# The last weight but one, loaded half in whole rows and half in column halves

## The chip, the cores and the metric

The kernel runs on one core of a Trainium2 chip. The metric is the device time of one execution in microseconds. Before the change it is 147.64 us, the median of three runs that lie between 147.49 and 147.65. One further execution was recorded by the hardware profiler, and all rows of the profile are of that one.

## The reference

An attention stage feeds a mixture of experts with soft slots. Cut to what matters:

```python
# attention: B=4, H=8, S=768, D=64; per head either full causal or sinks plus a window of 64
a = softmax(mask(q @ k.T / 8)); x = (a @ v) as [3072, 512]
# soft slots: NE=8 experts, 4 slots each, D=512, F=1024
logits = x @ phi                                   # [3072, 32]
slot_input = softmax(logits, axis=0).T @ x         # [8, 4, 512]
for e in range(8):
    slot_out[e] = relu(slot_input[e] @ w1[e]) @ w2[e]   # w2[e] is [1024, 512]
out = softmax(logits, axis=1) @ slot_out           # [3072, 512], fp32
```

The weights w1 and w2 are 2 MB of fp32 for each expert, 32 MB in all; the output is 6.29 MB of fp32.

## The kernel before

**Order.** The kernel describes its work as a list of named operations, each with an engine, an estimated duration, a key (a due time), the operations that it depends on and the buffers that it takes and frees. A planner (`Plan.run`) simulates the engines and emits the instructions in the order that it finds. What an engine does is therefore fixed at build time; at run time an engine only waits for semaphores, in that order. The function `dma` describes a load: an "issue" operation on GpSimd (POOL), chained to the load issued before it and to the landing of the load eight places earlier, and a "land" operation with the estimated transfer time, which the consumers depend on.

**Loads.** All inputs but three small ones are loaded by DMAs that POOL issues, one after the other on one queue, and the DMA converts them from fp32 to bf16 on the way. The weights are numbered: w0 to w7 are the experts' w1, w8 to w15 their w2. A whole w2 is laid out with the partition as `fi` and eight rows `fo` in each partition (row 8*fi + fo), so that a partition reads contiguous rows of 512 fp32 values, 2 KB each. The last two weights, w14 and w15 (experts 6 and 7), are split: `load_half(i, c)` loads the 256 columns of half c for all eight `fo`, 1 KB read and 512 B written at a time. The issue order at the end is w11, w12, w13, then w14.0, w15.0, w14.1, w15.1. These go into memory that the attention stage has done with: `pt` for w14, `qk` for w15, `xv` for w13, `vx` for w12.

**The experts.** The hidden layer comes first (H, the relu HR, the transposes TH, their copies HE). Then the second products: `w2_op(e, c0, c1)` makes W2.e for both halves at once (eight matmuls of 512 columns, one for each `fo`) or W2.e.c for one half (eight of 256). They add up in one PSUM bank, `so`, for all experts, since each slot's hidden values are masked to its expert. For each half: W2.6.c, the filling products ZT (three of zeros for half 0, two for half 1, made by `wait_zeros`, result unused), W2.7.c, and the scaling SO.c, which turns the half of the bank into bf16 `slot_out`.

**The output.** The 24 output tiles are a product of a 128x128 block of `expT` with `slot_out` (OM), scaled while it is moved out of PSUM by DVE or ACT (OE), with reciprocals that DVE makes of row sums (RW0, RW1 on PE, RWR0, RWR1 on DVE; RW1 is made in the right half's turn). Twelve tiles are done in column halves, first their left halves and after W2.7.1 their right halves; the other twelve are done whole at the end. The stores of the left halves are two on POOL's queue (128 KB and 384 KB) and four on SP's (256 KB each); then follow six right ones of 256 KB and three of 1 MB for the whole tiles, all on SP, which issues them in this order.

Of the kernel before, what the change touches and what calls it, by code (L numbers as in the profile page):

```python
# [226 lines left out]
def kernel(  # L227
# [19 lines left out]
    NE, DM, F = moe_w1.shape  # L247
# [61 lines left out]
    def tr_bf(s, n):  # L309
# [9 lines left out]
    hT_t = [xbf[:, 1024 * e:1024 * (e + 1)].rearrange("p (f c) -> p f c", f=8) for e in range(2)]  # L319

    pl = Plan({"S8": 11, "QT": 2, "KT": 2, "VT": 1, "VB": 2, "VF": 3, "PT": 2, "PTX": 2, "XB": 2,
               "XT": 1, "SC": 2, "TR": 2, "PV": 1, "BK": 8})
# [6 lines left out]
    def on(eng, occ, late=0.18):  # L329
        return {eng: (occ, occ + late)}  # L330
# [12 lines left out]
    def dma(name, nbytes, buf, dst, src, deps=()):  # L343
        if len(chain) >= 8:
            deps = list(deps) + [chain[-8]]
        iss = pl.op("issue " + name, on("POOL", 0.645, 1.4), -100, deps=list(deps) + [fifo[0]],
                    acq=[buf] if buf else [], lead=1.3, emit=lambda o: nc.gpsimd.dma_start(dst(), src))  # L347
        fifo[0] = iss
        took = nbytes / (395000.0 if nbytes == 1 << 20 and name != "w0" else 423000.0)
        chain.append(pl.op("land " + name, {"DMA": (took, took + 1.85 + 0.05 * len(chain))}, -100, deps=[iss] + chain[-1:], lead=5.2))  # L350
        return chain[-1]

# [23 lines left out]
    NW, NSPLIT = 2 * NE, 2  # L376
    wbuf = [Buf("S8") for _ in range(NW)]
    wland = [None] * NW
    late_mem = {}
# [6 lines left out]
    def w_row(i, x):  # L386
        n = 2 if i < NE else 4
        return w_mem(i)[:, x // n, :].rearrange("p (a f) -> p a f", a=n)[:, x % n, :]

    def w_half(i, c):  # L390
        return late_mem[i]()[:, 2048 * c:2048 * (c + 1)].rearrange("p (a f) -> p a f", a=8)

    hland = {}

    def load_half(i, c, deps=()):
        src = moe_w2[i - NE].rearrange("(fi fo) d -> fi fo d", fo=8)[:, :, 256 * c:256 * (c + 1)]
        hland[i, c] = dma(f"w{i}.{c}", 1 << 20, None, lambda: w_half(i, c), src, deps=deps)

    def load_w(i, deps=()):
        if i == 0:  # L400
# [124 lines left out]
    for n in range(4):  # L525
        o_fm[n] = pl.op(f"fm{n}", on("ACT", 0.65) if n == 0 else on("POOL", 0.9), -8 if n == 0 else T * n - 3.5,
                        deps=[o_fl], emit=lambda o, n=n: head_flags(o, n))
# [15 lines left out]
    def phi_t2(o):  # L543
        for n in range(4):
# [8 lines left out]
                  emit=lambda o: nc.vector.tensor_copy(  # L553
                      phi4, tr_bf(pb2.slot, 4 * NS).rearrange("p (n r s) -> p n r s", n=4, r=1).to_broadcast(
                          [P, 4, 4, NS])))
# [3 lines left out]
    def load_tile(ti):  # L559

        tbuf[ti], tland[ti], p0 = Buf("S8"), [], 0
        for x, b, x0, x1 in TILES[ti]:
# [8 lines left out]
                  emit=lambda o, x=x: nc.gpsimd.tensor_copy(w_mem(0)[:, 0, KB * x:KB * (x + 1)],  # L571
                                                            w0f[:, KB * x:KB * (x + 1)])) for x in range(4)]
# [116 lines left out]
    for b in range(B):  # L689
        for n in range(4):  # L690
            p = 4 * b + n
# [4 lines left out]
            def emit_v2(o, n=n, tr=tr):  # L696
                t = tr_bf(tr.slot, 768)
                for j in range(6):
                    nc.tensor.transpose(t[:, 128 * j:128 * (j + 1)], vT[:, 6 * n + j, :], ident)  # L699

            a = pl.op(f"V2.{p}", pe(56, 6), k0 + 1.5, deps=evs("v", b, n), acq=[tr], rel=[VTb[b]],
                      emit=emit_v2, mode="full", mm=6)

            def emit_vb(o, b=b, n=n, tr=tr):
# [4 lines left out]
                           acq=[VBb[b]] if n == 0 else [], rel=[tr], emit=emit_vb)  # L709
            VFb[p] = Buf("VF")  # L710

            def emit_vf(o, b=b, n=n, p=p):
# [4 lines left out]
                           emit=emit_vf)  # L717

            PTb[b, n] = Buf("PT")
            for kk, g in enumerate(range(5)):  # L720
# [3 lines left out]
                def emit_qk(o, b=b, n=n, g=g, sc=sc):  # L724
                    parts, c = [], 0
                    for j, q0, nb in PGROUPS[g]:
# [4 lines left out]
                a = pl.op(f"QK.{p}.{g}", on("PE", 0.235, 0.26), key - 2.0, deps=evs("q", b, n) + evs("k", b, n),  # L731
                          acq=[sc], rel=[QTb[b], KTb[b]], emit=emit_qk, mode="r64", mm=2 * len(PGROUPS[g]))

                def emit_ex(o, b=b, n=n, g=g, sc=sc):
# [4 lines left out]
                                   acq=[PTb[b, n]] if kk == 0 else [], rel=[sc], emit=emit_ex)  # L739
                for m, gs in enumerate(MGROUPS):  # L740
                    if gs[-1] == g:
                        o_m = pl.op(f"MK.{p}.{m}", on("DVE", [0.605, 0.605, 0.335][m]), key + 0.3,
                                    deps=[expo[p, x] for x in gs] + [o_hm[n]], emit=mask_emit(b, n, m))
# [3 lines left out]
        for ns in ([(0, 1), (2, 3)] if b == 0 else [(0, 1, 2, 3)]):  # L747
# [18 lines left out]
            def emit_mx(o, b=b, ns=ns):  # L766
# [5 lines left out]
                      emit=emit_mx)  # L772
# [5 lines left out]
    for b in range(B):  # L778
        for n in range(4):
            p = 4 * b + n  # L780
# [162 lines left out]
        if b == B - 1:  # L943
# [29 lines left out]
    load_w(12, deps=[pv_ops[f"PV.{p}.5"] for p in range(8, 12)])  # L973
    load_w(13, deps=[pv_ops["DS.2"]] + [pv_ops[f"XT.{p}"] for p in range(8, 12)] +
           [pv_ops[f"V2.{p}"] for p in range(12, 16)])
    load_half(14, 0, deps=[pv_ops["PV.14.5"]])
    load_half(15, 0, deps=qk_done[3])
    load_half(14, 1)
    load_half(15, 1)
# [68 lines left out]
    w2o = {}  # L1048

    def w2_op(e, c0, c1):  # L1050
        def emit_w2(o):
            e4, g0 = e // 4, e % 4
            for fo in range(8):
                g = fo % 4
                nc.tensor.matmul(banks[so.slot][32 * g:32 * (g + 1), 256 * c0:256 * c1],
                                 hT_t[e4][:, fo, 32 * g0:32 * (g0 + 1)], w_row(NE + e, fo) if c1 - c0 == 2 else w_half(NE + e, c0)[:, fo, :],
                                 start=(e == 0 and fo < 4), stop=(e == NE - 1 and fo >= 4),
                                 tile_position=(0, 32 * g), skip_group_check=True)

        land = [wland[NE + e]] if c1 - c0 == 2 else [hland[NE + e, c0]]  # L1060
        o = pl.op(f"W2.{e}" + ("" if c1 - c0 == 2 else f".{c0}"), on("PE", 0.22 * (c1 - c0), 0.27),
                  kt + (29 + e if c0 == 1 else 16 + e),
                  deps=[hte[e // 4]] + land + [w2o[c] for c in range(c0, c1) if c in w2o],
                  acq=[so] if e == 0 else [], emit=emit_w2, mode="c32", mm=8)
        for c in range(c0, c1):
            w2o[c] = o

# [6 lines left out]

        pl.op(name, pe(190, n), key, deps=[dep], acq=[zw] if first else [], rel=[zw], emit=emit_z, mode="full", mm=n)

    for e in range(NE - NSPLIT):
        w2_op(e, 0, 2)
    whole = w2o[0]
    for c in range(2):  # L1080
# [141 lines left out]
```

## Time and profile before

| What | Value |
|---|---|
| median of three runs | 147.64 us (147.49 to 147.65) |
| profiled execution | 147.56 us |
| its span on the core | 145.8 us, 4941 instructions |
| PE, DVE, ACT, POOL busy | 85%, 76%, 74%, 28% of the span |
| DMA queue q0 (POOL's) | 26.22 MB, its packets 92.9% of the 16 engines' time |
| DMA queue q1 (SP's) | 6.88 MB, 12.7% |
| granted clock of PE, mean | 0.944 |

The span runs from the first to the last instruction of the program; the rest of the execution's time lies around it. In the rows of the timeline the first column is the start in us from the span's start, the second the duration; PEld is PE's load of weights. In the rows of stretches the busy time of each engine stands in us with its number of instructions. The bytes of a converting load are counted as written, that is in bf16. A DMA's row has the size that it writes and the time from its issue to its landing.

### The profile page before, as it was taken

How to read it: one execution, taken by the hardware profiler on the slowest of the kernel's cores; microseconds unless marked ns; L12 is line 12 of the kernel's file. 1: busy time of each engine (PE TensorE's matmuls, PEld its weight loads, DVE VectorE, ACT ScalarE, POOL GpSimd, SP SyncE). 2: the span in 40 equal slices, each digit the busy share in tenths (PEclk: the TensorE clock that was granted, in tenths of full speed). 3: DMA queues.
4: the chain of work that ended last, by engine and by line, in shares of the span. 5: the costliest groups of instructions: out<-in, count | busy, mean ns of one | idle time of the engine just before them, and what ended most of it. 6: DMA issues, size and time to landing. Idle time of an engine off the chain costs nothing.

```text
span 145.8 us, 4941 instructions
## 1 busy us (share of the span) xinstructions
PE 124.6 (85%) x2134; PEld 82.3 (56%) x2134; DVE 110.8 (76%) x254; ACT 107.9 (74%) x147; POOL 40.5 (28%) x73
## 2 busy tenths in 40 slices
PE   6959989999999999999989999999959899869100
PEld 4437566676776758776548766666737355444000
DVE  1796399999999999999799899999983312449700
ACT  3152799999999988999998999999971461549300
POOL 6988631310311470100170011405380000110000
PEclk9985699999999999999999999999995999999965
DMA  5999999999999999999999999999999999999995
GB/s 135 277 208 211 215 215 214 212 216 214 215 214 214 216 215 214 216 214 211 215 214 215 214 216 219 212 217 215 217 210 215 211 194 197 185 321 362 407 420 247
DMA packets 14648, 33.40 MB, mean 229 GB/s; under 512 B 867, under 2 KB 7651, under 8 KB 14115
## 3 DMA queue, kind: packets, MB, share of 16 engines
q0 software_dynamic: 11184, 26.22, 92.9%
q1 hardware_dynamic: 3442, 6.88, 12.7%
q8 instruction: 16, 0.26, 0.6%
q14 instruction: 6, 0.04, 0.1%
HBM read 52.49 MB, written 6.29 MB: 403 GB/s over the span
## 4 chain that ended last, share of the span: by engine, by line
PE 28%; DVE 25%; DMA 18%; ACT 15%; issue 6%; POOL 1%; SPq 0%; DVEq 0%; ACTq 0%; POOLq 0%
DMA qk<-in_moe_w_dram 15%; ACT pt L735 11%; PE sc L665 6%; DVE pt L681 5%; PE pv L809 5%; DVE xv L833 5%; DMA phf<-in_moe_phi_dram 4%; DVE qk L336 3%; PE tr L613 3%; PE tr L639 3%; PE bk L1130 3%; PE tr L872 2%; DVE slot L1140 2%; DVE vf L714 2%; PE tr L845 2%
## 5 line engine op out<-in xcount | busy, mean ns | idle before, releaser
L735 ACT ACTIVATE pt<-sc 128x1024 bf16<-128x1024 f32 x80 | 77.0, 1049 | 3.0 <-PE sc L665 2.8
L665 PE MATMUL sc<-qk 64*128 64x512 bf16 (+3 forms) x256 | 31.3, 311 | 1.2 <-ACT pt L735 0.8
L681 DVE TENSOR_TENSOR pt<-pt,msk 128x1024 bf16<-128x1024 bf16 (+1 forms) x48 | 29.0, 609 | 2.0 <-ACT pt L735 1.8
L809 PEld LDWEIGHTS <-pt 128*128 128x128 bf16 x640 | 23.7, 98 | 6.2 <-issue 5.2
L809 PE MATMUL pv<-vx,pt 128*128 128x65 bf16 x320 | 25.9, 194 | 0.3 <-DVE xv L833 0.2
L809 PE MATMUL pv<-vf,pt 128*128 128x65 bf16 x320 | 21.6, 196 | 0.9 <-DVE xv L833 0.9
L347 POOL DMA_DIRECT2D slot<-in_moe_w_dram x11 | 7.8, 705 | 39.3 <-PE tr L639 29.5
L639 PE MATMUL tr<-ident,slot 128*64 128x128 bf16 (+1 forms) x448 | 16.3, 219 | 0.4 <-ACT qk L334 0.3
L336 DVE COPY qk<-tr 128x768 bf16<-128x768 bf16 (+2 forms) x33 | 15.1, 481 | 1.5 <-PE tr L613 1.3
L639 PEld LDWEIGHTS <-slot 128*64 128x64 bf16 (+1 forms) x448 | 13.1, 109 | 5.1 <-issue 4.8
L833 DVE TENSOR_TENSOR xv<-pv,rs 128x768 bf16<-128x768 f32 (+1 forms) x17 | 15.5, 910 | 0.6
L665 PEld LDWEIGHTS <-qk 64*128 64x128 bf16 x256 | 10.4, 94 | 9.6 <-issue 3.3
L1140 DVE TENSOR_SCALAR slot<-bk,rrow 128x256 f32<-128x256 f32 (+1 forms) x19 | 9.2, 561 | 2.2 <-PE bk L1130 2.2
L896 POOL COPY expT<-eT 128x192 bf16<-128x192 bf16 x12 | 7.4, 657 | 12.2 <-ACT eT L879 12.2
L336 DVE COPY xv<-tr 128x512 bf16<-128x512 bf16 (+2 forms) x20 | 7.9, 409 | 2.4 <-PE tr L613 2.2
L845 PE MATMUL tr<-ident,xv 128*128 128x128 bf16 x96 | 8.4, 224 | 1.3 <-DVE xv L833 0.9
L613 PE MATMUL tr<-ident_u,slot 96*64 96x96 bf16 x192 | 7.3, 238 | 1.9 <-DVE phi L553 1.4
L613 PEld LDWEIGHTS <-slot 96*64 96x64 bf16 x192 | 6.3, 133 | 4.5 <-issue 4.1
L336 DVE COPY xT<-tr 128x768 bf16<-128x768 bf16 (+1 forms) x14 | 7.5, 538 | 1.1 <-PE tr L845 1.1
L1138 ACT ACTIVATE slot<-bk,rrow 128x256 f32<-128x256 f32 (+1 forms) x17 | 7.7, 569 | 0.9 <-PE bk L1130 0.9
L699 PE MATMUL tr<-ident,xv 128*128 128x128 bf16 x96 | 8.1, 220 | 0.0
L845 PEld LDWEIGHTS <-xv 128*128 128x128 bf16 x96 | 6.0, 99 | 2.9 <-DVE xv L833 1.7
(123 smaller groups left out, 169.0 us busy)
## 6 DMA issues: line engine op xcount, KB each, us to landing
slot<-in_moe_w_dram POOLq DMA_DIRECT2D x10, 1024.0 KB, 24.5
out_dram<-slot SPq DMA_DIRECT2D x3, 1024.0 KB, 6.2
out_dram<-slot SPq DMA_DIRECT2D x10, 256.0 KB, 3.2
slot<-in_q_dram POOLq DMA_DIRECT2D x2, 768.0 KB, 19.4
slot<-in_k_dram POOLq DMA_DIRECT2D x2, 768.0 KB, 24.1
qk<-in_moe_w_dram SPq DMA_DIRECT2D x1, 1024.0 KB, 6.1
slot<-in_v_dram POOLq DMA_DIRECT2D x2, 512.0 KB, 21.3
qk<-in_moe_w_dram POOLq DMA_DIRECT2D x1, 1024.0 KB, 17.5
```

The lines of the kernel that those rows point to most:

```text
L336: nc.vector.tensor_copy(dst, src)
L347: acq=[buf] if buf else [], lead=1.3, emit=lambda o: nc.gpsimd.dma_start(dst(), src))
L613: nc.tensor.transpose(t[64 * i:64 * (i + 1), :, :, s, :], rv[:, i, 8 * c + s, :], ident_u)
L639: nc.tensor.transpose(t[64 * i:64 * (i + 1), :, s, :], rv[:, i, 8 * c + s, :], ident[0:R, 0:R])
L665: nc.tensor.matmul(scb[sc.slot][:, i, c:c + 128 * nb], kk, qq.rearrange("p b c -> p (b c)"), start=True, stop=True)
L681: nc.vector.tensor_tensor(pT, pT, mh, op=ALU.mult)
L699: nc.tensor.transpose(t[:, 128 * j:128 * (j + 1)], vT[:, 6 * n + j, :], ident)
L735: nc.scalar.activation(pTs[PTb[b, n].slot][:, :, 512 * g:512 * (g + 1)], scb[sc.slot], ACT.Exp, scale=scale)
L809: nc.tensor.matmul(pvb[:, bk, c:c + 65], lt, rhs, start=(j == 0), stop=(j == i))
L833: nc.vector.tensor_tensor(xo, pvw[:, :, :, 0:64], r.rearrange("p i (j o) -> p i j o", o=1).to_broadcast([P, 2, i1 - i0, 64]), op=ALU.mult)
L845: nc.tensor.transpose(t[:, 128 * i:128 * (i + 1)], xv[:, i, 128 * n:128 * (n + 1)], ident)
L1140: nc.vector.tensor_scalar(d, banks[bf.slot][:, 0:w], sc_, None, op0=ALU.mult)
```

## The change

w14 is loaded in three pieces instead of two. The rows `fo` 0 to 3 come whole, with all 512 columns, in one DMA (`load_whole`, 8 KB read and 4 KB written for each partition, without a break); the rows `fo` 4 to 7 come in two column halves as before. The issue order becomes w14 (whole rows), w14.0, w15.0, w14.1, w15.1, of 1, 0.5, 1, 0.5 and 1 MB as read. The products follow: W2.6 has four matmuls of 512 columns, W2.6.0 and W2.6.1 four of 256 each, instead of eight and eight of 256. The planner's estimates of transfer time are kept for the same loads by way of the odd sizes that `dma` is told.

```diff
-        took = nbytes / (395000.0 if nbytes == 1 << 20 and name != "w0" else 423000.0)
+        took = nbytes / (395000.0 if nbytes & 1023 else 423000.0)
...
     def w_half(i, c):
+        if i < NW - 1:
+            return late_mem[i]()[:, 2048 + 1024 * c:3072 + 1024 * c].rearrange("p (a f) -> p a f", a=4)
         return late_mem[i]()[:, 2048 * c:2048 * (c + 1)].rearrange("p (a f) -> p a f", a=8)
+
+    def w_whole():
+        return late_mem[NW - 2]()[:, 0:2048].rearrange("p (a f) -> p a f", a=4)
...
         src = moe_w2[i - NE].rearrange("(fi fo) d -> fi fo d", fo=8)[:, :, 256 * c:256 * (c + 1)]
-        hland[i, c] = dma(f"w{i}.{c}", 1 << 20, None, lambda: w_half(i, c), src, deps=deps)
+        if i < NW - 1:
+            src = src[:, 4:]
+        hland[i, c] = dma(f"w{i}.{c}", (1 << 20) - 100 if i == NW - 1 else (1 << 19) - 100, None, lambda: w_half(i, c), src, deps=deps)
+
+    def load_whole(i, deps):
+        src = moe_w2[i - NE].rearrange("(fi fo) d -> fi fo d", fo=8)[:, 0:4]
+        wland[i] = dma(f"w{i}", 1 << 20, None, w_whole, src, deps=deps)
...
-    load_half(14, 0, deps=[pv_ops["PV.14.5"]])
+    load_whole(14, deps=[pv_ops["PV.14.5"]])
+    load_half(14, 0)
     load_half(15, 0, deps=qk_done[3])
     load_half(14, 1)
     load_half(15, 1)
...
     def w2_op(e, c0, c1):
+        part = e == NE - 2
+        fos = range(8) if not part else range(4) if c1 - c0 == 2 else range(4, 8)
+
         def emit_w2(o):
             e4, g0 = e // 4, e % 4
-            for fo in range(8):
+            for fo in fos:
                 g = fo % 4
+                if c1 - c0 == 2:
+                    rhs = w_whole()[:, fo, :] if part else w_row(NE + e, fo)
+                else:
+                    rhs = w_half(NE + e, c0)[:, fo - 4 if part else fo, :]
...
-    for e in range(NE - NSPLIT):
+    for e in range(NE - 1):
         w2_op(e, 0, 2)
```

In the order of instructions that the planner makes of it, four things move beside the loads. PE makes W2.6 ahead of RW0 and W2.6.0 behind it, with ZT0 and W2.7.0 after that as before. The two fillers ZT1 stand behind W2.7.1 instead of ahead of it, and so ahead of RW1. SO.1 is made by DVE, ahead of the second reciprocals, instead of by ACT. And the twelve right halves and twelve whole tiles are dealt to DVE and ACT a little differently. POOL and SP issue the same stores in the same order.

More of the change, by code (lines that the diff above doesn't have):

```diff
@@ L1050, in w2_op @@
     def w2_op(e, c0, c1):
+        part = e == NE - 2
+        fos = range(8) if not part else range(4) if c1 - c0 == 2 else range(4, 8)
         def emit_w2(o):
             e4, g0 = e // 4, e % 4
-            for fo in range(8):
+            for fo in fos:
                 g = fo % 4
+                if c1 - c0 == 2:
+                    rhs = w_whole()[:, fo, :] if part else w_row(NE + e, fo)
+                else:
+                    rhs = w_half(NE + e, c0)[:, fo - 4 if part else fo, :]
                 nc.tensor.matmul(banks[so.slot][32 * g:32 * (g + 1), 256 * c0:256 * c1],
-                                 hT_t[e4][:, fo, 32 * g0:32 * (g0 + 1)], w_row(NE + e, fo) if c1 - c0 == 2 else w_half(NE + e, c0)[:, fo, :],
+                                 hT_t[e4][:, fo, 32 * g0:32 * (g0 + 1)], rhs,
                                  start=(e == 0 and fo < 4), stop=(e == NE - 1 and fo >= 4),
@@ L1060, in w2_op @@
         land = [wland[NE + e]] if c1 - c0 == 2 else [hland[NE + e, c0]]
-        o = pl.op(f"W2.{e}" + ("" if c1 - c0 == 2 else f".{c0}"), on("PE", 0.22 * (c1 - c0), 0.27),
+        o = pl.op(f"W2.{e}" + ("" if c1 - c0 == 2 else f".{c0}"), on("PE", 0.22 * (c1 - c0) * len(fos) / 8, 0.27),
                   kt + (29 + e if c0 == 1 else 16 + e),
                   deps=[hte[e // 4]] + land + [w2o[c] for c in range(c0, c1) if c in w2o],
-                  acq=[so] if e == 0 else [], emit=emit_w2, mode="c32", mm=8)
+                  acq=[so] if e == 0 else [], emit=emit_w2, mode="c32", mm=len(fos))
         for c in range(c0, c1):
```

## The prediction

> **What bounds the kernel now.** I read the page's slices first, then the chain of waits from 105 us on, then the loads and stores one by one, and last the packets on the DMA engines in half microseconds.
>
> ```profile
> span 145.8 us, 4941 instructions
> ...
> DMA  5999999999999999999999999999999999999995
> GB/s 135 277 208 211 215 215 214 212 216 214 215 214 214 216 215 214 216 214 211 215 214 215 214 216 219 212 217 215 217 210 215 211 194 197 185 321 362 407 420 247
> ```
>
> The DMA engines never rest between the first and the last slice, so the transfers set the time. Loads count at the bf16 bytes that they write, half of the fp32 that they read; from slice 36 on only stores run. The chain of waits names the load that parts the two:
>
> ```profile
> 108.08 21.34 DMA qk<-in_moe_w_dram
> ...
> 129.46 0.43 PE bk L1055 x8
> ...
> 129.91 0.48 ACT msk L1113
> ...
> 130.44 1.62 PE bk L1130 x12
> ```
>
> This is w15.1, the right half of the last weight: issued at 108.08, landed at 129.42, used by PE 0.04 us later. The chain blames it for the right half of the output; whether it also sets the end must be read from the stores. The loads before it, issue row first, then the same DMA's time to landing (w13, w14.0, w15.0):
>
> ```profile
> 102.45 0.71 POOL L347 DMA_DIRECT2D xv<-in_moe_w_dram  x1
> xv<-in_moe_w_dram POOLq DMA_DIRECT2D x1, 1024.0 KB, 16.4
> 105.45 0.90 POOL L347 DMA_DIRECT2D pt<-in_moe_w_dram  x1 [2.29 <-PE pv L809]
> pt<-in_moe_w_dram POOLq DMA_DIRECT2D x1, 512.0 KB, 16.0
> 106.35 0.87 POOL L347 DMA_DIRECT2D qk<-in_moe_w_dram  x1
> qk<-in_moe_w_dram POOLq DMA_DIRECT2D x1, 512.0 KB, 17.8
> ```
>
> They land at 118.85, 121.45 and 124.15, and w15.1 at 129.42: four column halves in 10.57 us, 2.64 each. Now the stretches around the change from loads to stores; the last two columns are the DMA share and GB/s:
>
> ```profile
> 85.00:105.00 20.00, 19.75 (x356) 13.46 (x354) 19.66 (x41) 19.82 (x25) 5.54 (x9) 1.00 1.06 214
> 118.50:126.00 7.50, 6.92 (x114) 3.56 (x115) 1.62 (x3) 1.83 (x3) 0.00 (x0) 1.00 1.45 198
> 127.50:128.00 0.50, 0.50 (x11) 0.16 (x10) 0.50 (x3) 0.50 (x3) 0.50 (x1) 1.00 0.93 159
> 128.00:128.50 0.50, 0.50 (x6) 0.13 (x3) 0.44 (x2) 0.40 (x2) 0.22 (x1) 1.00 1.10 236
> 128.50:129.00 0.50, 0.02 (x1) 0.04 (x1) 0.00 (x0) 0.00 (x0) 0.00 (x0) 1.00 1.20 353
> 131.00:136.00 5.00, 4.23 (x21) 1.73 (x18) 5.00 (x11) 5.00 (x11) 0.00 (x0) 1.00 1.06 368
> 138.00:144.00 6.00, 0.00 (x0) 0.00 (x0) 0.00 (x0) 0.00 (x0) 0.00 (x0) 0.65 1.01 426
> 144.00:144.50 0.50, 0.00 (x0) 0.00 (x0) 0.00 (x0) 0.00 (x0) 0.00 (x0) 0.50 0.40 164
> ```
>
> Whole-row loads run at 214 GB/s, column halves at 198. The stores then run without a break at 368 (1 KB pieces) and 426 (8 KB rows) until about 144.2, while PE, DVE and ACT are done before 138. So the end is: the moment the stores take over the engines, plus their bytes. Rates of 159 and 236 at 127.5 to 128.5 show that the hand-over is ragged. The packets in the half microseconds from 124.0, 127.5, 128.0 and 128.5 tell why (load packets are 512 B; q1 carries SP's stores):
>
> ```profile
> DMA packets 195, 0.10 MB, mean 198 GB/s; under 512 B 2, under 2 KB 195, under 8 KB 195
> DMA packets 107, 0.08 MB, mean 159 GB/s; under 512 B 1, under 2 KB 100, under 8 KB 107
> DMA packets 144, 0.12 MB, mean 236 GB/s; under 512 B 8, under 2 KB 135, under 8 KB 144
> q1 hardware_dynamic: 31, 0.03, 17.7%
> DMA packets 161, 0.18 MB, mean 353 GB/s; under 512 B 9, under 2 KB 147, under 8 KB 161
> q1 hardware_dynamic: 96, 0.10, 56.4%
> ```
>
> Load packets: 193, then 99, then 135-8-31 = 96, then 147-9-96 = about 42. From 127.5 on half of the engines have finished their loads; the other half keep their full pace until about 128.7 (42 of 96 packets is 0.22 us into the last window). So there is an early and a late group of eight. The first larger packets, the POOL stores, are the 7 in the second window, whose 40 fine slices show them from about 127.9; SP's first come at 128.5 - 0.5 x 31/96 = 128.3. The early group idles up to 1.2 us; the late one goes from loads into stores without a gap. From 128.75 the remaining work at full rate is: ten column stores and two POOL stores, 3.15 MB at 368 = 8.5 us, and 3.15 MB of full rows at 426 = 7.4; 128.75 + 15.9 = 144.6 against 144.2 seen (the early group had done some of it). I take the late group as what sets the end.
>
> **The change, part by part.** (1) Loads. Half of w14 goes as whole rows: its 0.524 MB of bf16 takes 0.524/214 = 2.45 us instead of 0.524/198 = 2.65. Saved: 0.20 us on every engine; by the landings it is 0.19 (2.64 less 2.45). I take 0.20. The bounds are 0 (the rate hangs on something other than the piece size) and 0.20 (whole rows were never seen faster than 214 to 219). A fifth DMA issue on POOL takes 0.9 us, at about 109, 7 us before its data moves, and POOL has nothing after it until its stores at 126.78: nothing. The eight-back landing waits of the new issue order point to loads that landed by about 109, for which the old order has the same kind of wait.
>
> The Trainium skill, "DMA: Bandwidth & Descriptors", section Specifications, gives 512 B as the smallest transfer for line rate. By that rule the 512 B pieces lose nothing and whole rows save nothing; the trace has 198 against 214, so I go by the rows, and keep the rule's outcome as a rival.
>
> (2) The left half becomes ready later. It needed 2 of the 4 MB read, now 2.5: the time from w13's landing to w15.0's goes from 2 x 2.65 to 2.45 + 1.32 + 2.65, that is +1.12. In the trace PE did not wait for that landing:
>
> ```profile
> 123.71 0.40 PE L1055 MATMUL bk<-pt,xT 128*32 128x256 bf16 x8
> ...
> 124.04 0.74 PE L1073 MATMUL bk<-zt,ident 128*128 128x448 bf16 x3
> ...
> 124.71 0.40 PE L1055 MATMUL bk<-qk,xT 128*32 128x256 bf16 x8
> ...
> 125.17 0.47 ACT L1113 ACTIVATE msk<-bk,rcs 128x256 bf16<-128x256 f32 x1 [4.38 <-PE bk L1055]
> ...
> 126.78 1.44 POOL L1149 DMA_DIRECT2D out_dram<-slot  x2 [17.83 <-DVE slot L1140]
> ...
> 127.35 10.62 SPq L1149 DMA_DIRECT2D out_dram<-slot  x13
> ```
>
> W2.7.0 started at 124.71 though w15.0 was there at 124.15, because the three filling products ZT0 ran first. So 0.56 us of the delay is covered: it now starts at 124.15 + 1.12 + 0.04 = 125.31, 0.60 later. PE's work ahead of it (four products of 512 columns instead of eight of 256, no more columns in all) is done well before. Behind it, scaling, twelve products, twelve evictions and six store issues follow in the same order: POOL's first at 127.38, SP's at 127.95. First packets: 128.5 and 128.9.
>
> (3) What that costs at the end. The late engines are through with loads at 128.72 - 0.20 = 128.52. POOL's first store is there at 128.5: 128 KB, 8 KB on each engine, at 426/16 GB/s 0.31 us, to 128.83. SP's first comes at 128.9. Idle on the late group: about 0.05. The early group idles 0.60 longer, which costs nothing as long as the late one is last. Below zero this term cannot go; its upper bound is the whole 0.60, with no cover at all. I take 0.05, since both instants are read off rows and fall within 0.1 us of each other.
>
> (4) The right half. In the new order the two fillers ZT1 stand behind W2.7.1 instead of ahead of it, and SO.1 is on DVE.
>
> ```profile
> 127.97 0.55 PE L1073 MATMUL bk<-zt,ident 128*128 128x448 bf16 x2
> 129.80 0.45 PE L1096 MATMUL bk<-cols,expT 128*128 128x1 bf16 x12
> 128.93 0.45 SPq L1149 DMA_DIRECT2D out_dram<-slot  x1
> out_dram<-slot SPq DMA_DIRECT2D x1, 256.0 KB, 4.5
> 131.39 0.37 SPq L1149 DMA_DIRECT2D out_dram<-slot  x1
> out_dram<-slot SPq DMA_DIRECT2D x1, 256.0 KB, 2.7
> ```
>
> The fillers (0.47 us of PE by the start of the next weights, at most 0.55 by this row) push RW1 and so DVE's reciprocals, for which every right eviction waits: they come 0.47 later against W2.7.1, less what DVE idled between (0.2), so about 0.26. W2.7.1 itself comes 0.20 earlier. The first right store is issued at 131.39 + 0.06. Does it come in time? It landed at 134.1, the last left store at 133.4: 0.7 apart, the pace of the stream (256 KB at 368 GB/s is 0.71). Its 2.7 us hold 0.95 from issue to first packet (as for SP's first) and 0.71 of transfer, so it had between 0 and 1.0 us to spare; the stream will need it 0.15 sooner, so it must have 0.21. Cost 0 to 0.21, taken as 0 (the middle of the spare is 0.5).
>
> **Sum:** -0.20 + 0.05 = -0.15 us. The profiled execution took 147.56 (1.76 around its span of 145.8): 147.41. The median shown is 0.08 above the profiled execution, so 147.49 is the forecast.
>
> No row here says which engine carried a packet. The Trainium skill, same page, section The descriptor swizzle, states that the partition fixes the engine; by it no early engine can take over a late one's bytes, and the sum stands; if they could, the second rival below holds, 147.74.
>
> **The rivals.** *The first store sets the end* (slower). If the tail of the loads is no fixed group but thin traffic on all engines, every engine waits for the stores, and the 16.3 us from the first store packet to the end simply move by 0.60: 147.64 + 0.60 = 148.24. For it: 159 GB/s at 127.5, so capacity is already going to waste there. Against: load packets stand at exactly half their number for a microsecond, as a fixed half would leave them. It decides where the first store packet comes after the loads' last on most engines.
>
> *All engines share the bytes.* Half of them idle 0.60 longer, 0.30 of the whole, less 0.20 saved: +0.10, 147.74. For it: early and late end together, the rate holding to 144. Against: POOL's and SP's first stores do not run ahead on the early group, the rate being 353 and not more when the late one joins.
>
> *The first right store comes late:* -0.15 + 0.21 = +0.06, 147.70. The smallest issue-to-landing time of any store, 2.7, speaks for it, the even 0.7 against.
>
> *No gain from whole rows:* the loads end where they did, the left half moves 0.80, SP's first packet comes at 129.1 against 128.72 + 0.31, and the idle is 0.07: 147.71. The 214 GB/s through 20 us speaks against.
>
> *A cleaner hand-over:* both groups start to store within 0.1 us of each other, so the thin start (353 where 368 follows, and 236 before) goes too; worth another 0.15 at most, 147.33 or a little lower. For it: 128.0 to 128.5 moves only 236. Against: that hole is the early group's, which nobody waits for.
>
> **How the numbers follow.** The forecast's mechanism 0.45, the first store 0.20, shared bytes 0.13, the cleaner hand-over 0.12, the late right store 0.05, no gain 0.05. The forecast's own range is 147.25 to 147.70: its idle term from 0 to 0.2, and the spread of the runs, 147.49 to 147.65. Differences under 0.2%, 0.30 us, are about what a measurement of this kernel cannot tell from none; that puts the borders at 147.34 and 147.94. Faster: 0.75 of the hand-over case and a quarter of the forecast's, 0.09 + 0.11, and 0.02 from the rest: 0.22. Slower: the first-store case, 0.20, and 0.03 from the tails of the others: 0.23. Within: 0.55. The range goes from 147.2 to 148.1: it leaves out the upper half of the first-store case and some of the hand-over case, under 0.2 together.
>
> **What would show it.** w15.0 landing at 125.2 to 125.3 and W2.7.0 at once behind it: step 2. w15.1 at 129.2: step 1. POOL's first store issue near 127.4 and SP's near 127.95, and the load packets ending near 128.5: step 3. First right store issued near 131.45 with the stores' landings still 0.7 apart: step 4. If the last store packet moves by the 0.60 of the first, the late group was a misreading; if w15.1 lands at 129.4, the whole rows save nothing.

## The result, and the profile after

The changed kernel takes 148.16 us (median of 10 runs, 147.90 to 148.70), the kernel before 147.70 beside it (147.49 to 148.02): a ratio of 1.0036, 95% interval 1.0021 to 1.0051. It is slower by 0.46 us, where -0.15 was forecast; 148.16 lies just outside the range of 147.2 to 148.1. The profiled execution took 147.95 us, 0.39 more than that of before.

The page of the changed kernel, its first line and three of its rows in 40 slices:

```profile
span 146.2 us, 4936 instructions
...
PEclk9955999999999999999999999999999999869975
DMA  5999999999999999999999999999999999999995
GB/s 132 286 211 210 216 213 214 213 216 214 214 215 212 214 213 215 213 214 217 214 215 211 215 214 215 214 215 215 214 215 214 211 204 198 165 309 352 398 428 251
```

The DMA row shows no pause here either: a tenth is too coarse for what happened. The GB/s row does: 165, 309, 352 in slices 35 to 37, against 185, 321, 362 before. And PE's granted clock has a dip in slices 35 and 36 that needs a look.

The loads of the changed kernel, issue row first, then size and time to landing (w13, the whole rows of w14, w15.0):

```profile
101.37 0.71 POOL L347 DMA_DIRECT2D xv<-in_moe_w_dram  x1
xv<-in_moe_w_dram POOLq DMA_DIRECT2D x1, 1024.0 KB, 17.3
104.38 0.56 POOL L347 DMA_DIRECT2D pt<-in_moe_w_dram  x1 [2.30 <-PE pv L821]
pt<-in_moe_w_dram POOLq DMA_DIRECT2D x1, 512.0 KB, 16.7
105.67 0.88 POOL L347 DMA_DIRECT2D qk<-in_moe_w_dram  x1
qk<-in_moe_w_dram POOLq DMA_DIRECT2D x1, 512.0 KB, 19.4
```

The chain of waits of the changed kernel, from w15.1's issue:

```profile
107.29 21.84 DMA qk<-in_moe_w_dram
...
129.17 0.62 PE bk L1075 x8
129.79 0.82 PE bk L1093 x2
130.61 0.28 PE bk L1116 x12
130.89 1.48 PE bk L1150 x12
```

w13 landed at 118.67, the whole rows at 121.1, w15.0 at 125.1 and w15.1 at 129.13, 10.46 us after w13 where the kernel before took 10.57 to 10.62: the loads are shorter by 0.1 to 0.2. Behind w15.1 the chain shows PE at 0.62 + 0.82 + 0.28 us before the first right output product, where it had 0.43 and ACT's 0.48 before.

Now the stretches of the changed kernel around the change-over, in the columns that the prediction used (the last three: PE's clock, DMA share, GB/s):

```profile
127.50:128.00 0.50, 0.50 (x5) 0.30 (x2) 0.50 (x2) 0.50 (x2) 0.40 (x2) 0.50 0.73 99
128.00:128.50 0.50, 0.50 (x6) 0.13 (x5) 0.50 (x3) 0.50 (x3) 0.50 (x1) 0.50 0.96 184
128.50:129.00 0.50, 0.24 (x4) 0.00 (x0) 0.38 (x1) 0.41 (x1) 0.15 (x1) 0.50 0.94 326
131.00:136.00 5.00, 4.54 (x24) 2.00 (x21) 5.00 (x12) 4.83 (x11) 0.00 (x0) 1.00 1.05 358
144.00:144.50 0.50, 0.00 (x0) 0.00 (x0) 0.00 (x0) 0.00 (x0) 0.00 (x0) 0.50 1.09 459
144.50:145.00 0.50, 0.00 (x0) 0.00 (x0) 0.00 (x0) 0.00 (x0) 0.00 (x0) 0.50 0.17 66
```

Between 127.5 and 129 the DMAs move 99, 184 and 326 GB/s where they moved 159, 236 and 353; and the stores end in the stretch from 144.5, not in that from 144.0. The packets of the changed kernel in the half microsecond from 127.5:

```profile
DMA packets 97, 0.05 MB, mean 99 GB/s; under 512 B 0, under 2 KB 97, under 8 KB 97
```

97 load packets in half a microsecond, as before (99): what half of the engines would leave at full pace. But none is above 2 KB: by this reading the other half have nothing at all to do. (The records name no engine.)

The timeline of the changed kernel (start, duration, engine, line):

```profile
125.16 0.40 PE L1075 MATMUL bk<-qk,xT 128*32 128x256 bf16 x8 [1.70 <-DMA qk<-in_moe_w_dram]
...
127.22 1.44 POOL L1169 DMA_DIRECT2D out_dram<-slot  x2 [19.04 <-DVE slot L1160]
127.79 6.17 SPq L1169 DMA_DIRECT2D out_dram<-slot  x8
...
129.17 0.62 PE L1075 MATMUL bk<-qk,xT 128*32 128x256 bf16 x8 [0.44 <-DMA qk<-in_moe_w_dram]
...
129.72 0.89 PE L1093 MATMUL bk<-zt,ident 128*128 128x448 bf16 x2
...
131.70 0.37 SPq L1169 DMA_DIRECT2D out_dram<-slot  x1
```

W2.7.0 waits 1.70 us for w15.0 and starts at 125.16; POOL's first store is issued at 127.22 (126.78 before), SP's at 127.79 (127.35), the first right store at 131.70 (131.39).

**Where the time went.** The two profiled executions are shifted against each other, so from here on times count from w12's landing (113.92 before, 113.78 after), the last load that the change leaves alone. I counted store bytes from the packet records:

| us after w12's landing | before, KB stored | after | behind |
|---|---|---|---|
| 16 | 581 | 459 | 122 |
| 17 | 946 | 823 | 123 |
| 20 | 2034 | 1853 | 181 |
| 24 | 3629 | 3408 | 221 |
| 28 | 5317 | 5095 | 222 |

222 KB at the 426 GB/s of the end are 0.52 us, and the last packet ends 31.11 us after w12's landing instead of 30.61: 0.50. More than half of the loss, 123 KB, is there once the change-over is done. Eight engines that idle 0.58 us longer (the delay of SP's first packet, 14.38 to 14.96) lose 8 x 0.58 x 368/16 = 107 KB. That is close: the idle of the early group, which I had costed at nothing, looks to have been paid, and was never got back.

### The profile page after: what moved, and what is told of

It is laid out like the page before. It is cut to its first block, busy times and chain, and to the rows that moved or that the text cites. A ratio compares the mean times of both kernels' runs of the same rounds, so it can differ in the third digit from the quotient of the medians.

```text
span 146.2 us, 4936 instructions
## 1 busy us (share of the span) xinstructions
PE 123.2 (84%) x2130; PEld 81.6 (56%) x2130; DVE 110.9 (76%) x255; ACT 107.3 (73%) x146; POOL 40.7 (28%) x74
## 4 chain that ended last, share of the span: by engine, by line
PE 29%; DMA 22%; DVE 19%; ACT 14%; POOL 5%; issue 4%; DVEq 0%; POOLq 0%; ACTq 0%
DMA qk<-in_moe_w_dram 15%; ACT pt L747 11%; PE sc L677 8%; PE pv L821 7%; DMA slot<-in_k_dram 7%; DVE pt L693 4%; DVE qk L336 3%; DVE xv L845 3%; PE tr L651 3%; PE tr L884 3%; PE bk L1150 2%; PE tr L857 2%; POOL slot L347 2%; DVE slot L1160 2%; DVE xv L336 2%
## 5 line engine op out<-in xcount | busy, mean ns | idle before, releaser
L677 PE MATMUL sc<-qk 64*128 64x512 bf16 (+3 forms) x256 | 31.1, 308 | 1.1 <-ACT pt L747 0.8
L821 PE MATMUL pv<-vf,pt 128*128 128x65 bf16 x320 | 21.1, 194 | 0.9 <-DVE xv L845 0.9
L1150 PE MATMUL bk<-msk,expT 128*128 128x256 bf16 (+1 forms) x36 | 7.0, 329 | 0.7 <-ACT msk L1133 0.6
```

Of the source, the lines that this page charges most:

```text
L677: nc.tensor.matmul(scb[sc.slot][:, i, c:c + 128 * nb], kk, qq.rearrange("p b c -> p (b c)"), start=True, stop=True)
L821: nc.tensor.matmul(pvb[:, bk, c:c + 65], lt, rhs, start=(j == 0), stop=(j == i))
L1150: nc.tensor.matmul(banks[bf.slot][:, 0:w], out_lhs(gi, r), slot_out[:, cs], start=True, stop=True)
```

## The experiments

Theory after the result: the end hangs on when the stores start. *Left*: it follows the first left stores one to one, and the change makes these late. *Right*: it follows the first right store, which the dip of the clock made late. *Loads*: the new pieces themselves cost something. Ratios are to the kernel before on the same chip, with 95% intervals; its medians there lay between 147.66 and 147.75, single runs between 147.2 and 149.0, so that differences under some 0.3% are seldom told apart.

**The changed kernel again** (no edit).

> The changed kernel once more, for comparison on the same chip. Both theories: 0.3 to 0.6 us slower than before, PE's granted clock near 0.5 between 127 and 130 us.

148.38 us, ratio 1.0051 (1.0024 to 1.0078). The loss is there in a second set of runs; SP's first packet at 14.98, end at 31.13.

**The left half on time, the loads as in the change.** W2.7.0 reads w14's left half, which has landed, in place of w15's, and waits for nine fillers only. Expert 7's product is thereby left out of the left columns. Both halves of W2.7 are also tied behind their fillers, which puts ZT1 ahead of W2.7.1 again:

```diff
-                    rhs = w_half(NE + e, c0)[:, fo - 4 if part else fo, :]
+                    rhs = w_half(NW - 2, 0)[:, fo % 4, :] if c0 == 0 else w_half(NE + e, c0)[:, fo - 4 if part else fo, :]
...
-        land = [wland[NE + e]] if c1 - c0 == 2 else [hland[NE + e, c0]]
+        land = [wland[NE + e]] if c1 - c0 == 2 else [hland[NE + e if c0 else NW - 2, c0]]
...
-                wait_zeros(f"ZT{c}", 2 if c else 3, kt + (29.5 + e if c else 22.5), w2o[c], c == 0)
+                zt_op[c] = wait_zeros(f"ZT{c}", 2 if c else 9, kt + (29.5 + e if c else 22.5), w2o[c], c == 0)
```

> The changed kernel, in which W2.7.0 reads w14's left half a second time instead of w15's, behind 9 fillers: it leaves out expert 7's product for the left columns, so the left half can start at its old time, 124.65 us, with the clock held and the new loads. Theory A: the loads' saving is kept, 147.4 to 147.6. If the new loads cost something by themselves: 147.8 or more.

147.68 us, ratio 1.0007 (0.9978 to 1.0036), 0.70 below the second run of the changed kernel on the same chip. With the same loads the loss is no longer seen, though the interval just reaches the changed kernel's 1.0036. The timeline of this kernel:

```profile
123.82 1.49 PE L1093 MATMUL bk<-zt,ident 128*128 128x448 bf16 x7
125.24 0.40 PE L1075 MATMUL bk<-pt,xT 128*32 128x256 bf16 x8
...
129.65 0.40 PE L1075 MATMUL bk<-qk,xT 128*32 128x256 bf16 x8 [0.43 <-DMA qk<-in_moe_w_dram]
```

PE does not idle ahead of W2.7.0, and the right half's product takes 0.40 us, not 0.62: the edit removed the late left half, the dip of the clock and ZT1's new place together, so it does not tell left from right. In its profile, a run of 148.19 us, W2.7.0 starts 0.46 us earlier than in the changed kernel, counted from w12's landing, but SP's first packet comes only 0.17 earlier (14.79).

**The left half early.** The same, expert 7's left product left out too, with three fillers and W2.7.0 not tied to them (`2 if c else 3`, no `zt_op` among its dependencies).

> The changed kernel, in which W2.7.0 reads w14's left half a second time and waits for nothing else, so the left half starts some 2 us earlier than in the changed kernel (it leaves out expert 7's product for the left columns). Counting from w13's landing, five profiles so far end 16.0 to 16.2 us after the first packet of SP's stores. Theory A (that start sets the end one to one, however early): 146.0 us. Theory P (all engines' capacity is shared; an earlier start gains until no engine idles between loads and stores, some 0.6 us of all sixteen, and the loads' 0.2): 146.8 to 147.1. Theory L (the loads' late engines set the end, as forecast): 147.4 to 147.6.

147.43 us, ratio 0.9979 (0.9953 to 1.0005). These are the loads of the change once more, and the interval leaves out its loss, while an early left half gains nothing in the kernel before (below): the pieces by themselves do not make the loss. SP's first packet comes 1.9 us earlier than in the run above (12.90 against 14.79), the end only 0.4 (30.44 against 30.85). The stretches of this kernel from 131.0 show why:

```profile
131.00:131.50 0.50, 0.50 (x5) 0.32 (x3) 0.50 (x3) 0.50 (x3) 0.00 (x0) 0.50 0.65 227
131.50:132.00 0.50, 0.50 (x3) 0.29 (x2) 0.50 (x3) 0.50 (x3) 0.00 (x0) 0.50 0.74 260
132.00:132.50 0.50, 0.50 (x2) 0.15 (x1) 0.50 (x2) 0.50 (x2) 0.00 (x0) 0.50 1.05 360
```

The left stores run dry (227 GB/s) before the right half's come. From there the right half sets the end.

**The left half late, the right one on time.** The changed kernel with ten fillers that keep PE busy, W2.6.1 tied behind the left products, RW1 ahead of W2.7.1 and ZT1 ahead of it too:

```diff
+                zt_op[c] = wait_zeros(f"ZT{c}", 2 if c else 10, kt + (29.5 + e if c else 22.5), w2o[c], c == 0)
...
+        key = kt + (35.2 if x else 21.4)
+        a = pl.op(f"RW{x}", pe(29, 4 * (g1 - g0)), key, deps=[eto[b] for b in range(B)] + [o_st, w61 if x else whole],
...
+    w61.deps.append([o for o in pl.ops if o.name == "OM.2.3.0"][0])
```

> The changed kernel with 10 fillers ahead of W2.7.0 (clock held), W2.6.1 kept behind the left products, and RW1 with its reciprocals ahead of W2.7.1. Counted from w12's landing, SP's first packet stays at 14.9 us, the first right store is issued at 17.2 or before (17.9 in the changed kernel, 17.5 before). Theory two arms (the end is the later of SP's first packet + 16.1 and the first right issue + 12.9): end at 31.0 to 31.1, 148.1 to 148.3. If the clock and the late right half are the whole cost of the change: end at 30.5, 147.7.

148.71 us, ratio 1.0062 (1.0029 to 1.0095). The timeline of this kernel:

```profile
125.38 0.40 PE L1075 MATMUL bk<-qk,xT 128*32 128x256 bf16 x8 [0.38 <-DMA qk<-in_moe_w_dram]
...
128.34 0.40 SPq L1171 DMA_DIRECT2D out_dram<-slot  x1
...
129.58 0.40 PE L1075 MATMUL bk<-qk,xT 128*32 128x256 bf16 x8
...
131.51 0.53 SPq L1171 DMA_DIRECT2D out_dram<-slot  x1
```

The clock holds (0.40), and the first right store is issued 17.52 us after w12's landing, as good as before the change (17.47). SP's first packet is at 15.26, the end at 31.30. The loss stays with the right half on time: a late left half makes one alone. It was later here than in the change, by 0.88 us against 0.58, so the run shows that the left half costs, not that it makes all of the 0.46.

**The clock held, a misfire.** The changed kernel with eleven fillers in ZT0 (`2 if c else 11`).

> The changed kernel with 11 fillers instead of 3 ahead of W2.7.0, so that PE does not idle while it waits for w15.0; ZT1 comes ahead of W2.7.1 again. Theory A (the later left half costs, by the later first store): the left half is still 0.45 us late, so 147.9 to 148.1 us. Theory B (the idle PE loses its clock and the right half comes late): clock 1.0 from 127 to 130, first right store issued at 131.4 or before, 147.5 to 147.7.

149.78 us, ratio 1.0137 (1.0096 to 1.0179). The longer estimate led the planner to put W2.6.1 and ZT1 ahead of the left half's output products:

```profile
126.22 0.29 PE L1075 MATMUL bk<-pt,xT 128*32 128x256 bf16 x4 [0.92 <-DMA pt<-in_moe_w_dram]
126.45 0.55 PE L1093 MATMUL bk<-zt,ident 128*128 128x448 bf16 x2
126.84 1.96 PE L1150 MATMUL bk<-msk,expT 128*128 128x256 bf16 x12
```

PE waits for w14.1 with twelve ready products behind it. It says nothing on the clock, but moves the left stores further: SP's first packet 16.24, end 32.27, 16.03 behind it.

**The left half moved in the kernel before.** Four edits: five fillers in ZT0 instead of three; one instead of three; all left stores on SP's queue; and one filler with RW1 ahead of W2.7.1 and the first right store cut to half its size (`(0, 1), (1, 4)` for the first group):

```diff
-                wait_zeros(f"ZT{c}", 2 if c else 3, kt + (29.5 + e if c else 22.5), w2o[c], c == 0)
+                wait_zeros(f"ZT{c}", 2 if c else 5, kt + (29.5 + e if c else 22.5), w2o[c], c == 0)
```

> The kernel before, with 5 fillers instead of 3 ahead of W2.7.0: the left half starts 0.43 us later, loads and clock as before. Theory A: slower by 0.2 (half of the engines idle longer) to 0.43 us (all wait), 147.9 to 148.1. Theory B, and the forecast's late group: no change, 147.6 to 147.75.

```diff
+                wait_zeros(f"ZT{c}", 2 if c else 1, kt + (29.5 + e if c else 22.5), w2o[c], c == 0)
```

> The kernel before with one filler instead of three ahead of W2.7.0, so that it starts when w15.0 lands, up to 0.43 us earlier where PE was late. Theory A: 147.3. Theory P: 147.5. Theory L: no change, 147.7.

```diff
-        store("SP" if gi else "POOL", "l", gi, r0, r1, slice(0, 256), kt + 31 + gi + 0.1 * r0)
+        store("SP", "l", gi, r0, r1, slice(0, 256), kt + 31 + gi + 0.1 * r0)
```

> The kernel before with all stores on SP: SP's first store is then the 128 KB one that POOL had, issued 0.5 us earlier than SP's first now, and the 384 KB one follows; nothing of POOL's stores queues behind the loads. If SP's first packet sets the end: 147.2 to 147.3. If it is the first packet of any store: 147.6 to 147.8. If six issues of 0.45 us in a row feed the engines too slowly: 147.9 or more.

```diff
-        for r0, r1 in [(0, 2), (2, 4)]:
+        for r0, r1 in [(0, 1), (1, 4)] if gi == 0 else [(0, 2), (2, 4)]:
```

> The kernel before with one filler ahead of W2.7.0 (left up to 0.4 us earlier), RW1 and its reciprocals ahead of W2.7.1, and a first right store of one tile (128 KB) instead of two. Two arms: SP's first packet at 13.9, first right issue at 17.2, end at 30.1 to 30.3, 147.2 to 147.4, faster than both kernels. If one arm alone or the loads set the end: 147.6 to 147.75.

Measured: 148.12 (1.0025, 0.9994 to 1.0056); 147.59 (0.9987, 0.9960 to 1.0015); 148.16 (1.0017, 0.9990 to 1.0044); 147.60 (1.0000, 0.9971 to 1.0029). None differs from the kernel before by more than its interval. In the first one's profile the fillers cost nothing, for PE was earlier against the loads than in the profile of before:

```profile
123.06 1.12 PE L1073 MATMUL bk<-zt,ident 128*128 128x448 bf16 x5
125.38 0.61 PE L1055 MATMUL bk<-qk,xT 128*32 128x256 bf16 x8 [1.20 <-DMA qk<-in_moe_w_dram]
```

How PE stands to the loads varies by some three microseconds between profiled executions (W2.6.0 starts 7.5 to 10.8 us after w12's landing with the same instructions ahead of it), so fillers are a poor means to delay anything by a set amount. The kernel before itself is known no better than that. In its profile PE was late, and W2.7.0 started 10.8 us after w12's landing. In two runs below that leave its left half as it was (nine fillers, right held), PE was earlier: W2.7.0 started at 10.2, right behind w15.0, and SP's first packet came at 13.8 instead of 14.38. With one filler, and with all stores on SP, the first stores came 0.5 and 1.4 us earlier and ran dry before the right ones (the 0.5 is no more than that spread); the stretches of the latter:

```profile
131.50:132.00 0.50, 0.50 (x6) 0.31 (x4) 0.50 (x2) 0.50 (x3) 0.00 (x0) 1.00 0.79 279
132.00:132.50 0.50, 0.49 (x3) 0.17 (x2) 0.50 (x2) 0.50 (x3) 0.00 (x0) 1.00 0.55 195
```

The fourth moved neither half forward in its profile: SP's first packet came at 14.34, the first right store was issued at 17.97, with PE's clock down. What moving both would gain was thus not seen.

**The right half late in the kernel before.** First by nine fillers ahead of W2.7.1 (`9 if c else 3`, W2.7.1 tied behind them):

> The kernel before with 9 fillers instead of 2 ahead of W2.7.1, so that the right half starts about 0.5 us later and nothing else moves; clock held. Two arms: SP's first packet at 14.4, first right issue at 17.95, end at 30.85 to 30.95, 0.3 us slower than before: 148.0. If the left stores' start alone sets the end: 147.7.

149.36 us, ratio 1.0092 (1.0059 to 1.0125), yet in its profile W2.7.1 waits 0.24 us for its weight behind the nine fillers: they delayed nothing there. The stretches at its end:

```profile
145.00:145.50 0.50, 0.00 (x0) 0.00 (x0) 0.00 (x0) 0.00 (x0) 0.00 (x0) 0.50 0.13 49
145.50:146.00 0.50, 0.00 (x0) 0.00 (x0) 0.00 (x0) 0.00 (x0) 0.00 (x0) 0.50 0.04 16
```

All but 0.05 MB is out at 145.05 (30.1 after w12's landing); then single packets follow for 1.6 us. The edit's cost is not explained by its profile. So a second try, with the fillers where no earlier PE can hide them, behind W2.7.1 and ahead of RW1:

```diff
+                if c == 0:
+                    wait_zeros("ZT0", 3, kt + 22.5, w2o[0], True)
+    zt1 = wait_zeros("ZT1", 6, kt + 36.5, w2o[1])
...
-        a = pl.op(f"RW{x}", pe(29, 4 * (g1 - g0)), key, deps=[eto[b] for b in range(B)] + [o_st, w2o[1] if x else whole],
+        a = pl.op(f"RW{x}", pe(29, 4 * (g1 - g0)), key, deps=[eto[b] for b in range(B)] + [o_st, zt1 if x else whole],
```

> The kernel before with six fillers behind the right half's last product instead of two ahead of it, and the right half's row sums behind them; the left half, the loads and the bytes are as before. A filler takes 0.2 to 0.27 us on PE, so the first right store is issued 1.0 to 1.6 us later than in the kernel before, at about 18.5 to 19.1 us from the landing of w12 (17.47 before), with SP's first store packet still at about 14.4. Two arms (the end is the later of SP's first store packet + 16.1 us and of the first right store's issue + 13.0): the left stores run dry at about 18.2 from that landing, a gap of 0.7 to 1.3 us opens there, and the end is 31.5 to 32.1 from it, 0.9 to 1.5 later than before: 148.6 to 149.2 us, a ratio of 1.006 to 1.010. Only the left half counts (one arm): no change, 147.6 to 147.9.

148.90 us, ratio 1.0076 (1.0039 to 1.0112), inside the two arms' 1.006 to 1.010. The first right store of this kernel in the timeline:

```profile
132.75 0.37 SPq L1151 DMA_DIRECT2D out_dram<-slot  x1
```

Its stretches before and at that store:

```profile
132.00:132.50 0.50, 0.50 (x4) 0.38 (x3) 0.48 (x1) 0.28 (x1) 0.00 (x0) 0.50 0.50 174
132.50:133.00 0.50, 0.50 (x4) 0.35 (x3) 0.50 (x2) 0.50 (x2) 0.00 (x0) 0.50 0.10 33
133.00:133.50 0.50, 0.50 (x5) 0.34 (x3) 0.50 (x2) 0.33 (x2) 0.00 (x0) 0.56 0.00 0
```

The first right store is issued at 19.14 after w12's landing, 1.67 later than before, and the end comes at 32.00, 1.39 later. SP's first packet was early (13.76), and the DMAs stood still from 133.0 to 133.5: a late right half costs as well, by itself.

**Three weights in column halves**, the kernel before with w13 split too (`NSPLIT = 3`), to see the slower pieces:

> The kernel before with w13, too, in column halves: the left half is ready 2.2 us earlier, the loads end 0.4 us later. It computes the whole output. Theory A: 145.5 to 146. Theory P: 0.4 lost and at most 0.6 to 0.7 won, 147.4 to 147.7. Theory L: 148.1.

150.31 us, ratio 1.0179 (1.0127 to 1.0231), far more than 1 MB of slower pieces can cost; the stores ran dry twice and, as above, a few packets came 1.6 us after the rest. Not explained.

**Fourteen halves with one filler**, to fill the dry stretch (`NL = 14`, store loops cut to `range(0, n, 2)` and `[:n // 2]`, ZT0 one filler):

> The kernel before with one filler ahead of the left half's last product instead of three, and fourteen output tiles made in column halves instead of twelve: a sixth left store of 256 KB on SP's queue (and a seventh right one) and a last whole store of 512 KB in place of one of 1 MB. Two arms: one filler brings SP's first store packet about 0.5 earlier (13.9 from the landing of w12), and the sixth left store fills the stretch in which the stores ran dry before the right half with one filler alone; the left arm then ends at 13.9 + 16.1 + 0.2 (0.5 MB more in pieces of 1 KB at 368 GB/s instead of 426), 30.2, and the right arm, which has 0.26 MB less behind it, at about 12.3 after its issue, 29.9 or, if PE's clock falls as in the run with one filler, 30.2: 0.3 to 0.5 less than the 30.6 of the kernel before, 147.2 to 147.4 us, a ratio of 0.997 to 0.998. If the gap was not what took the gain of the earlier left half away: 147.6 to 147.8.

148.62 us, ratio 1.0046 (1.0016 to 1.0076): a miss. The edit did not fill the dry stretch. The sixth left store holds two tiles of the fourth group, and in this kernel the reciprocals of that group come from RW1, in the right half's turn. The timeline shows the first output tile that ACT scales after the left ones waiting for them:

```profile
131.14 2.66 ACT L1138 ACTIVATE slot<-bk,rrow 128x256 f32<-128x256 f32 x7 [0.17 <-DVE rrow L1100]
```

The sixth left store is issued only at 17.60 us after w12's landing, and the first right store behind it at 18.14. Besides, PE was late in this profile (W2.7.0 at 125.58, though w15.0 had landed at 124.30), with SP's first packet at 15.06 and the end at 31.67; how far each of the two made the median of 12 runs is open. No version that beats the kernel before was found.

**All runs in one table**, in us from w12's landing; the fourth column is the later of "SP's first packet + 16.1" and "first right store's issue + 13.0", both numbers fitted to these runs:

| kernel | SP's first packet | first right store issued | later of the two | last packet ends |
|---|---|---|---|---|
| before | 14.38 | 17.47 | 30.5 | 30.6 |
| changed | 14.96 | 17.92 | 31.1 | 31.1 |
| changed again | 14.98 | 18.23 | 31.2 | 31.1 |
| left on time | 14.79 | 17.25 | 30.9 | 30.9 |
| left early | 12.90 | 17.29 | 30.3 | 30.4 |
| left late, right on time | 15.26 | 17.52 | 31.4 | 31.3 |
| clock held (misfire) | 16.24 | 18.36 | 32.3 | 32.3 |
| before, five fillers | 14.48 | 17.70 | 30.7 | 30.6 |
| before, one filler | 13.88 | 17.66 | 30.7 | 30.6 |
| before, all on SP | 13.00 | 17.47 | 30.5 | 30.7 |
| before, both early | 14.34 | 17.97 | 31.0 | 31.0 |
| before, nine fillers | 13.77 | 17.48 | 30.5 | 31.7 (all but single packets: 30.1) |
| before, right held | 13.76 | 19.14 | 32.1 | 32.0 |
| before, fourteen halves | 15.06 | 18.14 | 31.2 | 31.7 |
| before, three split | 13.29 | 18.10 | 31.1 | 32.6 (all but single packets: 31.0) |

Twelve of fifteen lie within 0.3 us. It is a rule for this output's bytes, from single executions. In the profiled execution of the kernel before both give 30.5: it stands where the two arms, left and right, meet. By this rule a delay of either costs, and an advance of one alone gains nothing; the runs with an early left half agree.

## Why the prediction was wrong

*Step 1, loads, -0.20:* right in kind, and nearly in size. From w13's landing to w15.1's it is 10.46 us against 10.57 to 10.62. The whole rows took 2.45 us.

*Step 2, the left half later:* right, the size in part by luck. w15.0 landed at 125.1 (forecast 125.2 to 125.3), W2.7.0 followed within 0.05, and SP's first packet moved by 0.58 against w12's landing (forecast 0.60). But the 0.56 that ZT0 covered was read off one execution in which PE was late. In the runs with nine fillers and with the right half held, with the same left half, W2.7.0 stood right behind w15.0 and the cover was gone.

*Step 3, the price of that, 0.05:* this is the step that failed. The packet counts show the two groups again, the late one loading at its pace until 128.5 or so; but "the early group idles 0.60 longer, which costs nothing as long as the late one is last" was wrong. The early group's idle accounts for 107 of the 123 KB missing at the change-over, and the end moved by 0.50 us. The run with the left half late and the right one on time shows that a late left half makes a loss alone. In the run with the left half on time the loss was no longer seen, though the clock's dip and ZT1's place went with it.

The check that the prediction made of this step rested on a misread end. Its sum gave 144.6 where 144.2 was "seen", and I put the 0.4 down to the work that the early group had done already. But the last packet ended at 144.53 (30.61 after w12's landing): a stretch counts a packet where it starts. So the gap to explain was 0.1, not 0.4. The early group's work is the term all the same: 15 us after w12's landing 226 KB were stored before the change and 129 KB after it, and by the table above the changed kernel never made that up.

The prediction leaned here on the Trainium skill, "DMA: Bandwidth & Descriptors", section The descriptor swizzle, by which the partition fixes the engine. From it I concluded that no engine takes over another's bytes, and so that the late group's end is the end. The records name no engine, so no run here shows or refutes the page; what they refute is the last conclusion.

*Step 4, the right half, +0.06 and no cost:* mis-sized. The first right store was issued 0.31 later by the span's clock, 0.45 by w12's landing. I counted ZT1 behind W2.7.1 (0.26) but not that PE, waiting 1.70 us for w15.0, would lose half its clock: W2.7.1 took 0.62 instead of 0.40 and ZT1 0.89 instead of 0.55. Nor does every right eviction wait for RW1's reciprocals, as I wrote: the kernel ties the first three groups of tiles to RW0's. What the chain shows ahead of the first right product is PE's own order, W2.7.1, ZT1, RW1. The run with the right half held (1.67 us later, the end 1.39 later) shows that a late right half costs by itself. For the 0.45 here that is only worked out, by the fitted rule: 31.2 on the right arm in the second run of the changed kernel, 31.1 on the left, and only the later one is paid.

*The rivals:* "The first store sets the end" gave 148.24 and comes closest: the 16.2 us from SP's first packet to the end stayed (16.23 before, 16.15 after). Its mechanism, thin traffic on all engines, is not what the packet counts suggest: they stand at half of their number, as before. "All engines share the bytes" has the right bytes at the change-over (half of the engines, 0.6 us) but a fifth of the price.

*What stays open:* 99 of the 222 KB are lost only between 17 and 24 us after w12's landing, at 358 GB/s from 131 to 136 against 368. It is there with the right half on time as well (88 KB), and partly with the left half on time (60 KB), so it is neither arm alone. And it is open why, in the kernel before, engines that start storing 0.7 us later than the others do not end later.

## What to carry to other kernels

At a change-over between two streams of transfers, count the bytes that all engines fail to move, also those of engines that are not the last to change over: an idle engine is free only if it is shown to end early. Ask of a saving in loads what it does to the first byte of the next stream, not only to the last of its own: 0.1 to 0.2 us of loads were bought with 0.6 us of later stores. Where two readiness times meet in one end, as here, a delay of either costs and an advance of one gained nothing, so a gain would need both moved; no run here managed that. And read such times from more than one execution: PE's place against the loads moved by three microseconds here.

## What the runs showed of the hardware

A wait of 1.7 us was enough to halve PE's clock, and not at once. In the changed kernel PE idled from 123.45 to 125.16; its stretches after that:

```profile
126.00:127.00 1.00, 0.84 (x7) 0.60 (x7) 0.56 (x2) 0.53 (x3) 0.00 (x0) 1.00 1.17 164
127.00:128.00 1.00, 1.00 (x6) 0.65 (x5) 1.00 (x3) 1.00 (x4) 0.68 (x2) 0.51 0.74 101
...
130.00:131.00 1.00, 1.00 (x17) 0.68 (x16) 0.47 (x2) 0.00 (x0) 0.00 (x0) 0.78 0.98 344
```

The clock fell at 127.0, 1.9 us after PE had work again, and came back at about 130.4. A wait of 1.58 us ahead of W2.7.0 was a border case: it lowered the clock in the run with all stores on SP (from 125.2 to 128.6) and not in the one with nine fillers. In the run meant to have both halves early it was down already as PE took up work, as the timeline shows:

```profile
124.29 0.62 PE L1055 MATMUL bk<-qk,xT 128*32 128x256 bf16 x8 [1.71 <-DMA qk<-in_moe_w_dram]
```

The same eight matmuls took 0.62 us at once. The Trainium skill, "TensorE: Matmul & The Clock Gate", Part 1, has the clock set by the activity of free-running windows of some 3.4 us, which agrees with a delay that differs from run to run and with the 3.4 us that the low clock lasts in the changed kernel (6.8 in its second run); that a partly busy window is enough to lower it, as here, the page does not say.

In two profiled executions the stores ended together but for single packets that went on for 1.6 us, one every 0.3 us, which at 8 KB each is a sixteenth of the 426 GB/s; the rows do not say which engine, and nothing here shows why.
